# Top-k attention and SoLU MLP on one core: the verdict's product goes ahead of the last four weight products, and these are cut into two column halves

## The chip, the cores and the metric

One core of a Trainium2 chip runs the whole program, once per launch. The metric is the device time of one execution in microseconds (us); a run's time is a little longer than the span of the profile, which goes from the first to the last of the program's own instructions.

## The reference

The inputs are q, k and v of shape (8 batches, 8 heads, 576 positions, 64), two weight matrices `moe_w_in` (512 x 1024) and `moe_w_out` (1024 x 512), and a gain vector.

```python
scores = scale * np.matmul(q, k.transpose(0, 1, 3, 2))
kth = np.partition(scores, -top_k, axis=-1)[..., -top_k:-top_k + 1]   # top_k = 32
scores = np.where(scores >= kth, scores, -1000000000.0)
attn = softmax(scores);  o = np.matmul(attn, v)
x = o.transpose(0, 2, 1, 3).reshape(4608, 512)
h = x @ w_in
solu = h * softmax(h)
ln = (solu - mean(solu)) / np.sqrt(var(solu) + 1e-06) * g_ln
out = ln @ w_out                                                      # 4608 x 512
```

`softmax` and `mean` stand here for the lines that the reference writes out. All of it is in single precision.

## The kernel before

The program has two paths. The fast path computes everything with a threshold search in place of an exact selection of the 32 largest scores. It collects seven conditions that must hold for its numbers to be valid (`w_passed`, L2643, one column of the tile `ok` each). At its end `w_verdict` (L2657) adds the columns with a TensorE product (`tp_ok`, L2659), and two small VectorE instructions (L2661, L2662) make the integer `bad`. Then every engine loads `bad` into a register (`values_load`, L2710) and branches on it (`tc.If`, L2712): with zero, the general path, some thousands of instructions long, is jumped over. With these inputs it is jumped over.

The attention part works in 32 steps over batches and query tiles of 128, and the MLP in 36 tiles of 128 tokens: four per batch, and one for the 64 last positions of two batches each. The stages of a token tile are work items with these names: `mm1` (x times `w_in`, L2567), `hexp`, `solu`, `square`, `spread`, `ln`, `transpose_ln` and `copy_ln` (which give `lnT`, the normalised tile transposed, L2617 and L2623), `mm2` in two items of four products each (L2628: `lnT` chunk c times the 128 rows c of `w_out`, eight products that add up in one PSUM bank `o_ps` of 128 x 512), `store` (ScalarE copies the bank to `osb`, L2635) and `send` (SyncE issues the DMA to the output, L2639). A tile of last positions is sent with two DMAs of 64 rows, since its rows belong to two batches. The last tile of the program is of this kind.

The order of the work is not that of the loops. `work_of` lists all items with a duration, what they come after and the buffers they use; `arranged` places them on the engines by that list and a table of ranks (`PLACES`), and returns them in order of their start. The program is then written in this order, each engine's instructions in its own queue. The tile framework adds the semaphore waits: an instruction that reads a tile waits for the earlier ones that wrote it, and an engine's semaphore is counted up by the last of a run of products rather than by each. In the order that results before the change, the last items on TensorE are the two `mm2` items of the last tile and then `w_verdict`; ScalarE ends with `store`, and SyncE with the two DMAs of `send`, after which come the load of `bad`, the branch and the program's closing instructions (L2712 and L2739).

Buffers that matter here: `o_ps` has two banks (`ps_o`), `osb` has one buffer (`p1`), and `tp_ok` takes one of the two `tp` banks.

Of the kernel before, what the change touches and what calls it, by code (L numbers as in the profile page):

```python
# [699 lines left out]
def arranged(work, rank):  # L700
    ops = work.ops
    prio = {k: rank(k) for k in ops}
    number = {k: n for n, k in enumerate(ops)}
    left = {k: len(set(o["after"])) for k, o in ops.items()}
    users = {k: [] for k in ops}
    still = {}
    for k, o in ops.items():
        for a in set(o["after"]):
            users[a].append(k)
        for u in set(o["uses"]):  # L710
            still[u] = still.get(u, 0) + 1
    free = {tag: [0] * n for tag, n in work.room.items()}
    ends = {}
    ready = dict.fromkeys(ops, 0)
    idle = dict.fromkeys(ENGINES, 0)
    waiting = {e: [] for e in ENGINES}
    for k, o in ops.items():
        if left[k] == 0:
            waiting[o["engine"]].append(k)
    held = {"DVE": 0, "POOL": 0}  # L720
    mode = "f"
    start = {}
    choice = {}
    while len(start) < len(ops):
        for e in ENGINES:
            if e in choice:
                continue
            found = []
            for k in sorted(waiting[e], key=lambda k: (prio[k], number[k]))[: 10 if e == "SP" else None]:
                s = max(idle[e], ready[k])  # L730
                if ops[k]["port"]:
                    s = max(s, held["POOL" if e == "DVE" else "DVE"])
                wanted = {}
                for u in ops[k]["uses"]:
                    if u not in ends:
                        wanted.setdefault(u[0], set()).add(u)
                for tag, us in wanted.items():
                    if len(free[tag]) < len(us):
                        break
                    at = free[tag][len(us) - 1]  # L740
                    s = max(s, at + HOP[e] if at else 0)
                else:
                    found.append((s, k))
            if found:
                soon = min(found, key=lambda x: x[0])[0] + PATIENCE[e]
                choice[e] = min(
                    (prio[k] + (TURNING if e == "PE" and ops[k]["mode"] != mode else 0), number[k], s, k)
                    for s, k in found if s <= soon
                )[2:]
        s, n, e = min((choice[e][0], n, e) for n, e in enumerate(ENGINES) if e in choice)  # L750
        k = choice[e][1]
        o = ops[k]
        if e == "PE":
            s += TURN.get((mode, o["mode"]), 0)
            mode = o["mode"]
        if o["port"]:
            held[e] = s + o["ns"]
        start[k] = s
        idle[e] = s + o["ns"]
        end = s + o["late"]  # L760
        for u in set(o["uses"]):
            if u not in ends:
                free[u[0]].pop(0)
            ends[u] = max(ends.get(u, 0), end)
            still[u] -= 1
            if still[u] == 0:
                free[u[0]] = sorted(free[u[0]] + [ends[u]])
        waiting[e].remove(k)
        for j in users[k]:
            other = ops[j]["engine"]  # L770
            ready[j] = max(ready[j], idle[e] if e == other == "PE" else end + HOP[other])
            left[j] -= 1
            if left[j] == 0:
                waiting[other].append(j)
        choice = {}
    return sorted(start, key=lambda k: (start[k], number[k]))
# [1007 lines left out]
def fast_path(  # L1784
# [25 lines left out]
    nc = tc.nc  # L1810
    B, H, S, D = q.shape
    NTOK, DM = out.shape
    DFF = moe_w_in.shape[1]
    NM = 4
# [4 lines left out]
    NF = DFF // P  # L1819
# [47 lines left out]
    parts = const.tile([P, 2, NT], F32, tag="parts", name="parts")  # L1867
# [9 lines left out]
    sum_all = const.tile([P, NTT], F32, tag="sum", name="sum_all")  # L1877
# [3 lines left out]
    w_out = const.tile([P, NF, DM], F32, tag="w_out", name="w_out")  # L1881
# [17 lines left out]
    def once(d, key, make):  # L1899

        if key not in d:
            d[key] = make()
        return d[key]
# [720 lines left out]

    def mm2(d, half):
        o = once(d, "o", lambda: ps_o.tile([P, 512], F32, tag="o", name="o_ps"))
        for c in range(half * NM, (half + 1) * NM):
            nc.tensor.matmul(  # L2628
                out=o, lhsT=d["lnT"][:, c, :], rhs=w_out[:, c, :],
                start=(c == 0), stop=(c == NF - 1),  # L2630
            )

    def store(d):
        d["osb"] = p1.tile([P, DM], F32, tag="osb", name="osb")
        nc.scalar.copy(out=d["osb"], in_=d["o"])  # L2635

    def send(d):
        for rows, dst in d["stores"]:
            nc.sync.dma_start(out=dst, in_=d["osb"][rows, :])  # L2639

# [26 lines left out]
    work, order_of_tokens = work_of(B, NP, steps, NF, w_wide)  # L2669
    tokens = []  # L2670
    for b, t, _, _ in order_of_tokens:
        rows = out[b * S : b * S + SM, :].rearrange("(p t) m -> p t m", t=NM)
        d = {"sum": sum_all[:, len(tokens) : len(tokens) + 1]}
        if t < NM:
            d["x"] = lambda b=b, t=t: xs["m", b, t // 2][:, :, t % 2 * P : (t % 2 + 1) * P]
            d["stores"] = [(slice(0, P), rows[:, t, :])]
        else:
            d["x"] = lambda b=b: xs["t", b // 2]
            d["stores"] = [
                (slice(m * ST, (m + 1) * ST), out[bb * S + SM : (bb + 1) * S, :])  # L2680
                for m, bb in enumerate((b - 1, b))
            ]
        tokens.append(d)
# [5 lines left out]
        chosen_sum, kth, kth_size, ends,  # L2689
        keep, inverse, spread_r, copy_s, turn_r, copy_r, rd_out, rd_in, transpose_p, copy_p, copy_pt, transpose_last, copy_last, attn_v, attn_t,  # L2690
        copy_v, mm1, hexp, solu, square, spread, ln, transpose_ln, copy_ln, mm2, store, send, load_g, turn_g,
        copy_g, load_w, w_bits, w_corr, w_sum, w_copy, w_gain, w_again, w_exp, w_check, w_passed,
        w_verdict,
    )}
    E = mybir.EngineType
    with tc.manual_schedule(engines={E.PE, E.Activation, E.DVE, E.Pool}):
        for kind, *args in arranged(work, place_of):
            if kind in TOKEN_KINDS:
                args[0] = tokens[args[0]]
            makers[kind](*args)  # L2700


@with_exitstack
def kernel(ctx: ExitStack, tc: tile.TileContext, *args):

    nc = tc.nc
    keep = ctx.enter_context(tc.tile_pool(name="keep", bufs=1))
    bad = keep.tile([1, 1], I32, tag="bad", name="bad")
    fast_path(tc, *args, bad)
    failed = nc.values_load(bad[0:1, 0:1], min_val=0, max_val=1,  # L2710
                            skip_runtime_bounds_check_because="a comparison's result")
    with tc.If(failed > 0):  # L2712
        general_path(tc, *args)
# [30 lines left out]
```

## Time and profile before

| | |
|---|---|
| three runs | 1193.06, 1195.21 and 1195.10 us (median 1195.1) |
| the profiled execution's own time | 1193.35 us |
| its span | 1191.5 us |
| mean granted TensorE clock | 0.991 |
| TensorE products busy | 1143.5 us, 96% of the span |
| VectorE busy | 1054.0 us, 88% |
| ScalarE busy | 1014.4 us, 85% |
| GpSimd busy | 154.4 us, 13% |
| `mm2` (L2628) on TensorE | 258.2 us in 576 products of 128x512 |
| `store` (L2635) on ScalarE | 21.1 us in 36 copies, 587 ns each |

A row of the timeline or of a group gives the engine, the line of the kernel, the operation, the tile written and the tiles read, and then partitions x elements. "Busy" of an engine does not count DMA issues, register loads, branches and semaphore waits; these are shown with a q behind the engine's name (SPq). The span is 1.85 us shorter than the profiled execution's own time; that part lies outside the program's own instructions.

### The profile page before, as it was taken

How to read it: one execution, taken by the hardware profiler on the slowest of the kernel's cores; microseconds unless marked ns; L12 is line 12 of the kernel's file. 1: busy time of each engine (PE TensorE's matmuls, PEld its weight loads, DVE VectorE, ACT ScalarE, POOL GpSimd, SP SyncE). 2: the span in 40 equal slices, each digit the busy share in tenths (PEclk: the TensorE clock that was granted, in tenths of full speed). 3: DMA queues.
4: the chain of work that ended last, by engine and by line, in shares of the span. 5: the costliest groups of instructions: out<-in, count | busy, mean ns of one | idle time of the engine just before them, and what ended most of it. 6: DMA issues, size and time to landing. Idle time of an engine off the chain costs nothing.

```text
span 1191.5 us, 18863 instructions
## 1 busy us (share of the span) xinstructions
PE 1143.5 (96%) x5868; PEld 648.2 (54%) x5868; DVE 1054.0 (88%) x3113; ACT 1014.4 (85%) x2180; POOL 154.4 (13%) x169
## 2 busy tenths in 40 slices
PE   6689999999999999999999999999999999999997
PEld 3345455555555555555555655555555555555553
DVE  4999999999899999899979998899989888999821
ACT  7899798999988898999896998999877989988642
POOL 1101101102021020202031010211013001120110
PEclk9799999999999999999999999999999999999999
DMA  7323111012110122111120112111020101102521
GB/s 202 97 75 92 43 34 48 13 49 54 59 26 28 33 63 65 37 45 40 51 54 12 40 49 68 31 41 52 30 76 18 42 21 40 59 11 91 173 76 30
DMA packets 110408, 64.55 MB, mean 54 GB/s; under 512 B 89421, under 2 KB 97882, under 8 KB 110298
## 3 DMA queue, kind: packets, MB, share of 16 engines
q1 hardware_dynamic: 110298, 63.25, 18.8%
q8 instruction: 49, 0.80, 0.3%
q14 instruction: 61, 0.50, 0.1%
HBM read 53.65 MB, written 9.57 MB: 53 GB/s over the span
## 4 chain that ended last, share of the span: by engine, by line
PE 50%; DVE 27%; ACT 17%; issue 3%; POOL 2%; DMA 0%; DVEq 0%; ACTq 0%; POOLq 0%
PE o_ps L2628 14%; PE h_ps L2567 9%; PE s_ps L2216 9%; ACT sg L2291 7%; PE tp_p L2470 6%; PE om L2526 6%; DVE junkv L2234 6%; DVE w L2323 5%; DVE w L2312 5%; DVE E L2393 3%; ACT PT L2483 2%; DVE solu L2586 2%; ACT X L2227 2%; PE tp_ln L2617 2%; PE om L2535 2%
## 5 line engine op out<-in xcount | busy, mean ns | idle before, releaser
L2628 PE MATMUL o_ps<-w_out,lnT 128*128 128x512 f32 x576 | 258.2, 594 | 0.2
L2567 PE MATMUL h_ps<-w_in,xTm 128*128 128x512 f32 x512 | 229.2, 593 | 0.0
L2323 DVE MAX8 w<-w 128x8 f32<-128x288 f32 x576 | 223.3, 445 | 0.2
L2291 ACT ACTIVATE sg<-X,t 128x576 bf16<-128x576 f32 x256 | 196.4, 774 | 12.0 <-DVE t L2276 10.8
L2312 DVE SCALAR_TENSOR_TENSOR w<-X,al,sg 128x576 f32<-128x576 f32 x256 | 200.7, 813 | 0.8
L2393 DVE SCALAR_TENSOR_TENSOR E<-X,kth,E 128x576 f32<-128x576 f32 x256 | 199.1, 815 | 1.6
L2227 ACT ACTIVATE X<-s_ps 128x576 f32<-128x576 f32 x256 | 160.2, 661 | 25.0 <-PE s_ps L2216 22.5
L2234 DVE TENSOR_SCALAR_CACHE_REDUCE junkv<-X,t 128x576 bf16<-128x576 f32 x216 | 174.6, 808 | 7.6 <-ACT X L2227 1.5
L2216 PE MATMUL s_ps<-kT,qT 64*128 64x288 f32 x1024 | 169.1, 438 | 9.8 <-ACT X L2227 4.4
L2628 PEld LDWEIGHTS o_ps<-w_out,lnT 128*128 128x128 f32 x576 | 105.1, 190 | 112.4 <-issue 110.1
L2470 PE MATMUL tp_p<-ident,E 128*128 128x128 f32 x1024 | 153.1, 278 | 7.9 <-DVE E L2393 2.9
L2483 ACT COPY PT<-tp_p 128x512 f32<-128x512 f32 x256 | 147.0, 591 | 12.4 <-PE tp_p L2470 11.9
L2470 PEld LDWEIGHTS tp_p<-ident,E 128*128 128x128 f32 x1024 | 116.3, 141 | 65.4 <-issue 31.8
L2348 ACT ACTIVATE E<-X 128x1152 f32<-128x1152 f32 x128 | 149.1, 1183 | 1.4 <-PE tp_p L2470 1.2
L2567 PEld LDWEIGHTS h_ps<-w_in,xTm 128*128 128x128 f32 x512 | 93.3, 190 | 98.1 <-issue 95.7
L2526 PE MATMUL om<-PT,vm 128*64 128x320 f32 (+1 forms) x1024 | 136.1, 411 | 1.0 <-ACT osb L2635 0.9
L2186 POOL TENSOR_TENSOR zs<-zs,phalf 128x9 f32<-128x9 f32 x32 | 63.6, 1989 | 520.2 <-DVE zs L2180 520.2
L2216 PEld LDWEIGHTS s_ps<-kT,qT 64*128 64x128 f32 x1024 | 85.7, 186 | 68.3 <-issue 22.2
L2526 PEld LDWEIGHTS om<-PT,vm 128*64 128x64 f32 x1024 | 69.9, 136 | 54.6 <-issue 10.6
L2602 POOL TENSOR_SCALAR var<-var 128x1 f32<-128x1 f32 x36 | 13.0, 361 | 490.3 <-ACT e_sb L2596 490.1
L2596 ACT ACTIVATE e_sb<-solu,nmu 128x1024 f32<-128x1024 f32 x36 | 41.5, 1153 | 23.1 <-DVE nmu L2590 21.8
L2578 ACT ACTIVATE e_sb<-h_ps 128x1024 f32<-128x1024 f32 x36 | 36.7, 1020 | 20.0 <-PE h_ps L2567 19.7
(146 smaller groups left out, 1503.9 us busy)
## 6 DMA issues: line engine op xcount, KB each, us to landing
km<-in_k_dram SPq DMA_DIRECT2D x32, 256.0 KB
q_sb<-in_q_dram SPq DMA_DIRECT2D x64, 128.0 KB
vm<-in_v_dram SPq DMA_DIRECT2D x32, 256.0 KB
out_dram<-osb SPq DMA_DIRECT2D x32, 256.0 KB
scales<-rows SPq DMA_DIRECT2D x58, 128.0 KB
w_raw<-in_moe_w_in_dram SPq DMA_DIRECT2D x8, 512.0 KB
w_raw<-in_moe_w_out_dram SPq DMA_DIRECT2D x8, 512.0 KB
w_again<-in_moe_w_in_dram SPq DMA_DIRECT2D x8, 512.0 KB
```

The costliest lines, as they stand in the source:

```text
L2216: nc.tensor.matmul(out=s[:, n, 0:SH], lhsT=queries_of(i, t)[hd, :], rhs=kT[hd, k0 : k0 + SH], start=True, stop=True,)
L2227: nc.scalar.activation(out=x, in_=st[i].pop(("s", j))[:, :, 0:SH], func=AF.Copy, scale=scale,)
L2234: nc.vector.tensor_scalar(out=junk, in0=x_of(i, j), scalar1=st[i][t][:, j : j + 1], scalar2=None, op0=ALU.is_ge, op1=ALU.add, accum_out=co ...
L2291: nc.scalar.activation(out=d["sg", j], in_=x_of(i, j), func=AF.Sign, scale=-(1.0 + 2.0**-23), bias=d["t1"][:, j : j + 1], accum_out=column ...
L2312: nc.vector.scalar_tensor_tensor(out=w, in0=x_of(i, j), scalar=d["al"][:, j : j + 1], in1=d.pop(("sg", j)), op0=ALU.subtract, op1=ALU.mult,)
L2323: nc.vector.max(w8[:, j, 8 * half : 8 * half + 8], w[:, half * SH : (half + 1) * SH])
L2393: nc.vector.scalar_tensor_tensor(out=e, in0=x_of(i, j), scalar=d["kth"][:, j : j + 1], in1=e, op0=ALU.is_ge, op1=ALU.mult, accum_out=den_a ...
L2470: nc.tensor.transpose(tp[:, c, :], e[:, c * P : (c + 1) * P], ident)
L2483: nc.scalar.copy(out=dst, in_=st[i].pop(("tp", j)))
L2526: nc.tensor.matmul(out=o[h * D : (h + 1) * D, cols], lhsT=vm[:, h, c, :], rhs=pt[:, h * NM + c, :], start=(c == 0), stop=False,)
L2567: nc.tensor.matmul(out=h[:, half, :], lhsT=x[:, c, :], rhs=w_in[:, c, half * 512 : (half + 1) * 512], start=(c == 0), stop=(c == NP - 1),)
L2628: nc.tensor.matmul(out=o, lhsT=d["lnT"][:, c, :], rhs=w_out[:, c, :], start=(c == 0), stop=(c == NF - 1),)
```

## The change

Three things are changed, all at the end of the program. `w_verdict` is taken out of its place in the order and put ahead of the last `mm2` item, the one with the last four products. In that item each of the four products of 512 columns becomes two of 256: first the four of columns 0 to 255, then the four of columns 256 to 511. For that tile `store` makes two copies of 256 columns, and behind each of them in the program stand the DMAs of that column half, so there are four DMAs of 64 rows x 256 columns where there were two of 64 x 512. All other tiles have one part and keep their form.

```diff
     def mm2(d, half):
         o = once(d, "o", lambda: ps_o.tile([P, 512], F32, tag="o", name="o_ps"))
-        for c in range(half * NM, (half + 1) * NM):
-            nc.tensor.matmul(
-                out=o, lhsT=d["lnT"][:, c, :], rhs=w_out[:, c, :],
-                start=(c == 0), stop=(c == NF - 1),
-            )
+        parts = d["parts"] if half else [slice(0, DM)]
+        for m in parts:
+            for c in range(half * NM, (half + 1) * NM):
+                nc.tensor.matmul(
+                    out=o[:, m], lhsT=d["lnT"][:, c, :], rhs=w_out[:, c, m],
+                    start=(c == 0), stop=(c == NF - 1 and m == parts[-1]),
+                )
 
     def store(d):
         d["osb"] = p1.tile([P, DM], F32, tag="osb", name="osb")
-        nc.scalar.copy(out=d["osb"], in_=d["o"])
+        for m in d["parts"]:
+            nc.scalar.copy(out=d["osb"][:, m], in_=d["o"][:, m])
+            if len(d["parts"]) > 1:
+                out_of(d, m)
+
+    def out_of(d, m):
+        for rows, dst in d["stores"]:
+            nc.sync.dma_start(out=dst[:, m], in_=d["osb"][rows, m])
 
     def send(d):
-        for rows, dst in d["stores"]:
-            nc.sync.dma_start(out=dst, in_=d["osb"][rows, :])
+        if len(d["parts"]) == 1:
+            out_of(d, d["parts"][0])
...
-        d = {"sum": sum_all[:, len(tokens) : len(tokens) + 1]}
+        d = {"sum": sum_all[:, len(tokens) : len(tokens) + 1], "parts": [slice(0, DM)]}
...
-        for kind, *args in arranged(work, place_of):
+        order = [k for k in arranged(work, place_of) if k[0] != "w_verdict"]
+        last = max(n for n, k in enumerate(order) if k[0] == "mm2")
+        tokens[order[last][1]]["parts"] = [slice(0, DM // 2), slice(DM // 2, DM)]
+        order.insert(last, ("w_verdict", 0))
+        for kind, *args in order:
```

## The prediction

> **What bounds the kernel now.** TensorE is busy for 96% of the span, but the change touches only the last 10 us, so I read the end of the profile. First the chain of waits over the last 20 us:
>
> ```profile
> 1172.97 0.87 PE tp_ln L2617 x8
> 1173.85 10.32 PE o_ps L2628 x24
> 1184.16 0.03 ACTq L2635
> 1184.19 0.04 issue
> 1184.23 0.59 ACT osb L2635
> ```
>
> TensorE runs 24 products on end and only the copy of the last bank follows. But the span ends at 1191.5, 6.7 us after this copy, and none of that counts as busy. So the second view is the timeline after 1184:
>
> ```profile
> 1184.08 0.19 PE L2659 MATMUL tp_ok<-ok,ones 128*1 128x7 f32 x2
> 1184.23 0.59 ACT L2635 COPY osb<-o_ps 128x512 f32<-128x512 f32 x1 [6.33 <-PE o_ps L2628]
> 1184.31 0.15 DVE L2661 TENSOR_REDUCE n_ok<-tp_ok 1x1 f32<-1x7 f32 x1 [8.87 <-PE tp_ok L2659]
> 1184.50 0.14 DVE L2662 TENSOR_SCALAR bad<-n_ok 1x1 int32<-1x1 f32 x1
> 1184.84 1.13 SPq L2639 DMA_DIRECT2D out_dram<-osb  x2
> ```
>
> `bad` is there at 1184.64, before the copy ends. Third, the lines of the register load (L2710), the branch and its landing (L2712), and the closing (L2739):
>
> ```profile
> L2710 ACTq TENSOR_LOAD <-bad x1: 462/462/462, 1184.7 to 1184.7; - x1
> L2710 SPq TENSOR_LOAD <-bad x1: 848/848/848, 1186.0 to 1186.0; - x1
> L2712 SPq EVENT_SEMAPHORE  x8: 17/17/17, 1189.6 to 1190.2; - x8
> L2712 DVEq EVENT_SEMAPHORE  x1: 21/21/21, 1189.1 to 1189.1; - x1
> L2712 PEldq EVENT_SEMAPHORE  x1: 51/51/51, 1189.8 to 1189.8; - x1
> L2739 SPq DRAIN x3: 7/7/13, 1190.7 to 1191.1; - x3
> ```
>
> The columns after x are shortest, median and longest ns, then first and last start. All engines but SyncE load `bad` at 1184.7. SyncE is at 1186.0 only, because its two DMA issues stand ahead in its queue. It branches until 1187.0, goes on at 1189.62 (2.6 us later), steps through 16 semaphore waits until 1190.7, and the closing barrier, in which all others already stand, ends the span. So the path that sets the end is: last product, copy, SyncE's issues (1.13), load (0.85), branch and restart (2.7), closing (1.9). The verdict isn't on it: `bad` had been ready for 1.39 us when SyncE came to read it.
>
> **The change part by part.**
>
> *The verdict earlier.* Its last input, a column of `ok`, is written at 1175.4, and the item would now stand near 1182.4, so it waits for nothing, and `bad` comes some 1.7 us earlier. VectorE and GpSimd, idle by then, branch earlier; ScalarE and TensorE can't before their last copy and products; none of the four ends the span. Gain on the path: nothing. The cost is on TensorE: two tiny products between full ones. Three rows price it. `tp_ok` starts 0.52 us after the last full product (1183.56 to 1184.08), where full ones follow at 0.429: 0.09. Its second pass starts 0.03 later. And the first full product after tiny ones pays for an uncovered weight load:
>
> ```profile
> 1057.97 0.16 PE L2172 MATMUL est<-stats,qTt 128*128 128x1 bf16 x1
> 1058.00 2.39 PE L2628 MATMUL o_ps<-w_out,lnT 128*128 128x512 f32 x5
> ```
>
> Five products take 2.39 us where 4 x 0.429 + 0.592 makes 2.31: 0.08, and it starts 0.03 after the tiny one. Sum 0.23 us; bounds 0.06 (the two tiny steps alone) and 0.4 (also a bare load of 0.19). At the end, where `tp_ok` stood, nothing is saved: the copy waited for the product before it.
>
> *The halves.* Products of 128x256 follow each other at 0.215 us in the trace (`om` L2535), so eight take 1.72 us and four full ones 1.72: zero. What should bring something is that the first half's copy starts while the second half is computed. The changed program, built but not run, says no: it gives the first 256-column copy a wait on TensorE's count after the eighth product, and the second copy no wait on TensorE. The semaphore is counted up only at the last of the eight. So the first copy starts where the full one did. A shorter copy is a gain all the same:
>
> ```profile
> L2635 ACT COPY osb<-o_ps 128x512 f32<-128x512 f32 x36 | 21.1, 587 | 24.6 <-PE o_ps L2628 18.6 <-issue 6.0
> L2509 ACT COPY PT<-tp_pt 128x256 f32<-128x256 f32 x32 | 12.2, 380 | 1.9 <-PE tp_pt L2505 1.9
> ```
>
> The first DMA may be issued 587 - 380 = 0.21 us earlier. The second copy ends some 0.25 later (copies of 512 columns follow at 0.47) and hides behind SyncE's first two issues.
>
> *Four DMAs.* SyncE issued the two 64-row DMAs in 0.49 and 0.59 us with 0.055 between them, and other pairs of such stores show 0.495 to 0.540 and 0.590 to 0.596. That an issue of 64 rows doesn't shrink with its bytes shows in the loads of 64 rows x 256 B (L2044: median 0.547 of 64). Two more are 2 x (0.59 + 0.055) = 1.29, and a separate wait ahead of the third 0.05: 1.34. Behind them in SyncE's queue wait its load of `bad` and its branch, and all engines wait for these in the barrier. Bounds: 0.8 (at the shortest store issue, 0.343) to 1.4.
>
> The Trainium skill prices this otherwise: "DMA: Bandwidth & Descriptors", section "Anatomy of one DMA — SWDGE (gpsimd) path", puts the sequencer's dispatch at about 50 ns of a fixed 2 us per DMA, for another issuing path. By that two more issues are 0.1 and the whole sum would be about 0.2 us. The trace's 0.49 and 0.59 per issue on SyncE say otherwise, and I go by them.
>
> *What comes after.* SyncE's load of `bad` (0.85) could come down to the 0.46 of ScalarE, which had no DMA ahead: 0 to -0.39; I take 0, because SyncE again comes from its own issues. The restart after the branch took 2.6 us on SyncE and 3.3 to 4.4 on the others, so I leave it; the earlier branches of two engines may relieve it by some tenths, not counted.
>
> *Sum:* 0.23 - 0.21 + 1.34 = +1.4 us (bounds 0.06 - 0.21 + 0.8 - 0.39 = +0.3 and 0.4 - 0.21 + 1.4 = +1.6). The profiled execution would go from 1193.35 to 1194.7. The four known times of before (1193.06, 1193.35, 1195.10, 1195.21) spread over 2.1 us, and the profiled one is 1.75 below the median of the runs. I lay the sum on the mean of the four, 1194.2: 1195.6.
>
> **The rivals.** A measurement of this kernel can tell about 0.2%, 2.4 us, from no change.
>
> *The last store decides (slower).* SyncE's closing waits include the stores' arrival. In the trace's semaphore updates the first store is complete at 1187.39 and the second at 1189.59, 2.2 us apart, and SyncE read that semaphore at 1189.71: 0.12 us to spare. If each further store adds 2.2, the fourth arrives at 1187.45 + 6.6 = 1194.05, and with the 1.6 us of closing after it the span ends at 1195.7: +4.2, profiled 1197.5. It decides from an arrival after 1191.2, about 4.4 us after the fourth issue; from 1192.2 on the kernel is slower beyond 0.2%. For it: only stragglers made the second store late, and there will be twice as many packets. Against: the bytes are the same, and at half the spacing the fourth store arrives at 1190.8, which costs nothing.
>
> *The halves do overlap.* Then the first copy starts four products (0.86) earlier, SyncE issues the first pair during the second half, and the third issue starts at about 1185.2: the issues end at 1186.4 in place of 1186.0, +0.5 us. Against it stands the built program's wait. The Trainium skill, "PSUM — Partial Sum Buffer", section "PSUM bank collisions raise a hardware error", says that an engine's read and TensorE's write of one bank must be kept apart even at other columns, which speaks against this overlap too; no run here shows it.
>
> *The tail shrinks (faster).* If SyncE's load falls to 0.46 and the earlier branches of the others save it up to half of its 2.6 us restart, the sum is 1.4 - 0.4 - 1.3 = -0.3. Even this stays within 0.2%; to be faster by 2.4 us, 3.8 would have to vanish from a tail of 7.3.
>
> **How the numbers follow.** My forecast 0.58, of which 0.03 comes out beyond 0.2% by the scatter of the runs; the late store 0.22; overlap 0.05; the shrunken tail 0.08; anything else 0.07, split 0.05 faster and 0.02 slower. So slower 0.03 + 0.22 + 0.02 = 0.27, same 0.55 + 0.05 + 0.08 = 0.68, faster 0.05. The range goes from the lowest time of before with the lower bound of the sum (1193.06 + 0.3 = 1193.4) to the mean with the late store's whole price (1194.2 + 4.2 = 1198.4).
>
> **What would show it.** In the changed profile: the first 256-column copy starts after the eighth short product; the eight together take 1.7 us; `tp_ok` opens a gap of about 0.2 us in the row of products; SyncE shows four issues over 2.4 us, its load of `bad` starts about 3.0 us after the end of the last product in place of 1.9, and its first L2712 wait comes 2.6 us after its branch. The prediction is wrong if the first copy starts 0.9 us before the last product ends, if the issues get shorter with the rows' bytes, or if a closing wait of SyncE stands for longer than 17 ns, which is the late store.

## The result, and the profile after

The changed kernel takes 1196.59 us against 1194.38 us, medians of 19 runs each. The ratio is 1.0015, with a 95% interval of 1.0008 to 1.0022: 1.8 us slower, between 1.0 and 2.6 (the medians differ by 2.2). One run of the changed kernel, of 1662.57 us at a granted clock of 0.654, counts in its median and not in the ratio. The profiled execution of the changed kernel took 1194.25 us, its span is 1192.5 us and its granted clock 0.990. It is the quickest of the 19, 0.9 us ahead of the next. The rows below are those of this execution; what the others lost beyond it can't be seen in them.

The lines below answer to those shown of before. First the end of the chain of waits of the changed kernel (start in us, length in us, what):

```profile
1172.68 0.87 PE tp_ln L2617 x8
1173.55 6.87 PE o_ps L2630 x16
1180.42 0.12 PE tp_ok L2668 x2
1180.54 3.67 PE o_ps L2630 x16
1184.21 0.03 ACTq L2638
1184.24 0.04 issue
1184.28 0.37 ACT osb L2638
```

`tp_ok` now stands inside the row of products, and the first 256-column copy starts behind all sixteen passes of the short products, not behind eight of them. From the first of the last eight transposes to the first copy it is 1184.28 - 1172.68 = 11.60 us; before it was 1184.23 - 1172.97 = 11.26. I call the stretch from that transpose to the end of the span the tail. With the spans to the hundredth, as the traces have them, it is 1192.46 - 1172.68 = 19.78 us after and 1191.54 - 1172.97 = 18.57 before, 1.2 us more. (The expectations below say 18.5 for before, from the rounded span.)

The timeline of the same stretch, with the DMA issues, which the chain leaves out:

```profile
1178.54 1.88 PE L2630 MATMUL o_ps<-w_out,lnT 128*128 128x512 f32 x4
1180.35 0.19 PE L2668 MATMUL tp_ok<-ok,ones 128*1 128x7 f32 x2
1180.47 3.72 PE L2630 MATMUL o_ps<-w_out,lnT 128*128 128x256 f32 x16
1184.28 0.65 ACT L2638 COPY osb<-o_ps 128x256 f32<-128x256 f32 x2 [6.67 <-PE o_ps L2630]
1184.67 2.47 SPq L2644 DMA_DIRECT2D out_dram<-osb  x4
```

The last product ends at 1180.47 + 3.72 = 1184.19. SyncE's issues take 2.47 us where two took 1.13; in the trace they are 0.492, 0.588, 0.605 and 0.587 long. The two copies are over at 1184.93, ahead of the third issue.

The third view is the register load (L2723), the branch and its landing (L2725) and the closing (L2752). After the x stand shortest, median and longest ns, and then first and last start in us:

```profile
L2723 PEldq TENSOR_LOAD <-bad x1: 485/485/485, 1181.0 to 1181.0; - x1
L2723 ACTq TENSOR_LOAD <-bad x1: 462/462/462, 1184.3 to 1184.3; - x1
L2723 SPq TENSOR_LOAD <-bad x1: 739/739/739, 1187.2 to 1187.2; - x1
L2725 SPq COMPARE_BRANCH  x1: 50/50/50, 1188.0 to 1188.0; - x1
L2725 SPq EVENT_SEMAPHORE  x8: 17/17/17, 1190.5 to 1191.1; - x8
L2725 PEldq EVENT_SEMAPHORE  x1: 51/51/51, 1185.3 to 1185.3; - x1
L2752 SPq DRAIN  x3: 7/7/13, 1191.6 to 1192.0; - x3
```

SyncE comes to read `bad` at 1187.2, 3.0 us after the last product, goes on behind its branch at 1190.5, and has stepped through its waits at 1191.6, where its drains begin. All other engines have landed by 1187.5 (ScalarE the last of them), so SyncE alone ends the span. TensorE read `bad` at 1181.0, when fourteen of the sixteen passes had still to start.

### The profile page after: what moved, and what is told of

It is laid out like the page before. It is cut to its first block, busy times and chain, and to the rows that moved or that the text cites. A ratio compares the mean times of both kernels' runs of the same rounds, so it can differ in the third digit from the quotient of the medians.

```text
span 1192.5 us, 18883 instructions
## 1 busy us (share of the span) xinstructions
PE 1143.6 (96%) x5876; PEld 649.7 (54%) x5876; DVE 1054.0 (88%) x3113; ACT 1013.8 (85%) x2181; POOL 154.3 (13%) x169
## 4 chain that ended last, share of the span: by engine, by line
PE 56%; DVE 22%; ACT 16%; issue 2%; POOL 2%; DMA 0%; DVEq 0%; ACTq 0%; POOLq 0%
PE o_ps L2630 15%; PE h_ps L2567 11%; PE s_ps L2216 9%; PE tp_p L2470 7%; PE om L2526 6%; ACT sg L2291 6%; DVE junkv L2234 5%; DVE w L2312 4%; DVE w L2323 4%; DVE E L2393 3%; PE tp_ln L2617 2%; ACT PT L2483 2%; PE om L2535 2%; ACT X L2227 2%; DVE solu L2586 2%
## 5 line engine op out<-in xcount | busy, mean ns | idle before, releaser
L2630 PE MATMUL o_ps<-w_out,lnT 128*128 128x512 f32 (+1 forms) x584 | 258.5, 588 | 0.3
L2348 ACT ACTIVATE E<-X 128x1152 f32<-128x1152 f32 x128 | 149.1, 1183 | 1.4 <-PE tp_p L2470 1.2
```

Source lines behind the costliest of these rows:

```text
L2630: nc.tensor.matmul(out=o[:, m], lhsT=d["lnT"][:, c, :], rhs=w_out[:, c, m], start=(c == 0), stop=(c == NF - 1 and m == parts[-1]),)
```

## The experiments

Every kernel is the changed one with the edit shown, unless it says otherwise, and was timed in five rounds against the kernel before, in three batches on three chips, each with its own runs of before. The tail is the stretch defined above, from one profiled execution.

| kernel | ratio to before, 95% interval | tail, us |
|---|---|---|
| before | 1 | 18.6 |
| the change | 1.0015 [1.0008, 1.0022] | 19.8 |
| verdict moved, whole parts | 1.0002 [0.9993, 1.0011] | 18.9 |
| halves, verdict in its old place | 1.0008 [0.9999, 1.0017] | 20.7 |
| quarters | 1.0032 [1.0021, 1.0043] | 23.6 |
| halves, two stores of whole rows | 0.9999 [0.9990, 1.0008] | 18.8 |
| halves in two banks | 0.9998 [0.9989, 1.0007] | 18.5 |
| one store on each queue | 1.0005 [0.9996, 1.0014] | 18.7 |
| the same, verdict moved | 0.9999 [0.9990, 1.0008] | 18.3 |
| two banks, one store of each half on each queue | 1.0001 [0.9992, 1.0010] | 18.1 |
| both stores from ScalarE | 1.0001 [0.9992, 1.0010] | 18.5 |
| the same, verdict moved | 0.9992 [0.9983, 1.0001] | 18.1 |
| two banks, all four stores from ScalarE, verdict moved | 0.9988 [0.9979, 0.9997] | 17.9 |
| no branch | 0.9972 [0.9962, 0.9982] | 15.9 |

**The verdict alone.** The parts are left whole:

```diff
-        tokens[order[last][1]]["parts"] = [slice(0, DM // 2), slice(DM // 2, DM)]
```

> Only the verdict is moved ahead of the last four weight products; these keep their 512 columns, and there is one copy and two DMAs as before. The tail is measured from the start of the last eight transposes (tp_ln) to the end of the span: 18.5 us before, 19.8 after the whole change. My theory: the verdict is not on the path that sets the end, so its place brings nothing by itself. It costs TensorE 0.3 us between the products, and the earlier branches of VectorE and GpSimd give back up to 0.26 (SyncE's register load and restart were 0.11 and 0.15 shorter in the changed profile): tail 18.4 to 18.8, time within 0.5 us of before. Rival, the verdict's place alone makes the loss: tail 19.5 or more. Rival, the early verdict is a real gain that the halves throw away: tail below 18.0.

The two ends of the stretch, from the chain of waits of this kernel:

```profile
1173.42 0.87 PE tp_ln L2617 x8
1185.00 0.58 ACT osb L2638
```

From the last eight transposes to the copy it took 11.58 us, 0.32 more than before, and the tail grew by the same 0.3, to just above what was expected. The end of SyncE's row, from the groups of this kernel:

```profile
L2722 SPq TENSOR_LOAD <-bad x1: 850/850/850, 1186.8 to 1186.8; - x1
L2724 SPq COMPARE_BRANCH  x1: 50/50/50, 1187.7 to 1187.7; - x1
L2724 SPq EVENT_SEMAPHORE  x8: 17/17/17, 1190.4 to 1190.9; - x8
```

Load and restart are those of before (0.85 us, and 2.6 from the branch to the first wait behind it). That TensorE, VectorE and GpSimd read `bad` and branch 3.4 us earlier, counted from the last eight transposes, gives SyncE nothing. So this part costs only its gap in the row of products, about a quarter of the loss, which the times alone don't tell from nothing.

**The halves alone.** The verdict goes back to its place:

```diff
-        order = [k for k in arranged(work, place_of) if k[0] != "w_verdict"]
+        order = list(arranged(work, place_of))
...
-        order.insert(last, ("w_verdict", 0))
```

> Only the halves: the last four weight products in 256-column halves, two copies, four DMAs; the verdict stays behind the last product. My theory: two more DMA issues on SyncE (1.34) less the shorter first copy (0.21): tail 18.5 + 1.1 = 19.6, time +1.1 us on before. The first copy starts after the last product as in the whole change. Rival (the loss comes from the verdict's place): tail 18.5. Rival (the last store's arrival decides): one of SyncE's closing waits is longer than 17 ns, and the tail is over 20.

The tail was 20.7, a microsecond over what was expected, and one row says where it lies (timeline of this kernel):

```profile
1184.25 3.60 SPq L2644 DMA_DIRECT2D out_dram<-osb  x4
```

Three of the four issues took 0.492, 0.588 and 0.547 us, the fourth 1.774, about 1.2 too much. The other terms came out as expected. In the times (1.0008) no extra microsecond shows, but they don't exclude one, and this execution (1195.03 us) was quicker than the median of its kernel (1195.49). Whether the other runs have the long issue too is not known. The last section comes back to it.

**Quarters.** If the issues behind the last copy carry the loss, four more of them should cost about as much each:

```diff
-        tokens[order[last][1]]["parts"] = [slice(0, DM // 2), slice(DM // 2, DM)]
+        tokens[order[last][1]]["parts"] = [slice(n * P, (n + 1) * P) for n in range(4)]
```

> The whole change with four column quarters instead of two halves: 128-column products, four copies, eight DMAs of 64 rows x 128 columns. A dose for the price of a DMA issue. My theory: an issue costs SyncE 0.59 + 0.055 us whatever its bytes, so four more issues and two more separate waits add 4 x 0.645 + 0.1 = 2.7, the first copy is 0.08 shorter: tail 19.8 + 2.6 = 22.4, time about +2.6 us on the changed kernel. Rival (an issue costs by its bytes, total bytes being the same): tail 19.8. Rival (the last store's arrival decides, 2.2 us per store): tail 26 or more, with a long closing wait on SyncE.

The kernel was 3.8 us slower than before, where the halves cost 1.8. Its issues in the timeline:

```profile
1186.03 6.00 SPq L2644 DMA_DIRECT2D out_dram<-osb  x8
```

Six more issues than before take 6.00 - 1.13 = 4.87 us. One of them lasted 1.50; without its extra 0.9 that is 0.66 for each. The tail is 1.2 over what was expected: the long issue is 0.9 of that, and a restart of 2.73 us most of the rest. Rows of 512 bytes cost SyncE what rows of 2 KB do. The price is that of these stores of 64 rows: the stores of whole tiles, 128 rows and twice the bytes, were issued in 0.34 to 0.37 us in 27 of 32 cases in the kernel before, the others in 0.45 to 0.60. The same run speaks on the stores' arrival: by the trace's semaphore updates the eight stores are complete between 1187.95 and 1193.34, 2.3 us before SyncE lands behind its branch at 1195.66. More stores don't arrive later than SyncE gets there, because SyncE itself is later.

**Halves without the extra stores.** Both copies are kept, and two DMAs of whole rows follow the second:

```diff
         for m in d["parts"]:
             nc.scalar.copy(out=d["osb"][:, m], in_=d["o"][:, m])
-            if len(d["parts"]) > 1:
-                out_of(d, m)
...
-        if len(d["parts"]) == 1:
-            out_of(d, d["parts"][0])
+        out_of(d, slice(0, DM))
```

> The whole change, but behind the two half copies stand two DMAs of the full width, as before the change, in place of four. My theory: this takes back the 1.34 of two issues, and the first issue comes 0.27 later, after both copies: tail (start of the last eight transposes to the end of the span; 18.5 before, 19.8 after, 18.9 with the verdict alone moved) 18.9 to 19.0, time within 1 us of before. SyncE's register load should be 0.85 again if it goes by the stores behind which it stands (two of 2 KB rows), 0.74 if it goes by something else in the change. Rival (the split copies or products are what costs): tail 19.5 or more.

With verdict and halves in place and only the two added DMAs gone, the loss is gone within the interval: 0.9999, and a tail 0.3 over that of before, as with the verdict alone. The timeline row and the load of this kernel:

```profile
1186.36 1.13 SPq L2642 DMA_DIRECT2D out_dram<-osb  x2
```

```profile
L2720 SPq TENSOR_LOAD <-bad x1: 840/840/840, 1187.5 to 1187.5; - x1
```

The load is at 0.84 again. It was 0.84 to 0.85 in the three kernels whose last stores have rows of 2 KB (before and the verdict alone are the others), and 0.73 to 0.74 in the four with narrower rows on SyncE, whether the verdict stood early or late: the 0.11 us that the change wins here come with its stores ahead of the load. These are narrower and there are more of them, and no run separates the two.

**A bank for each half.** Now the first copy really may start early, since the second half adds up in another PSUM tile. All eight products of the last tile are cut into halves here, not the last four alone:

```diff
-        o = once(d, "o", lambda: ps_o.tile([P, 512], F32, tag="o", name="o_ps"))
-        parts = d["parts"] if half else [slice(0, DM)]
-        for m in parts:
+        once(d, "o", lambda: ps_o.tile([P, 512], F32, tag="o", name="o_ps"))
+        if len(d["parts"]) > 1:
+            once(d, "o2", lambda: ps_big.tile([P, 2, 512], F32, tag="big", name="o2_ps"))
+        for n, m in enumerate(d["parts"]):
+            o = d["o2"][:, 0, :] if n else d["o"]
...
-                    start=(c == 0), stop=(c == NF - 1 and m == parts[-1]),
+                    start=(c == 0), stop=(c == NF - 1),
...
-            nc.scalar.copy(out=d["osb"][:, m], in_=d["o"][:, m])
+            o = d["o2"][:, 0, :] if m.start else d["o"]
+            nc.scalar.copy(out=d["osb"][:, m], in_=o[:, m])
```

> The whole change, but all eight products of the last tile are made in column halves, and the second half adds up in a PSUM bank of its own, so that the first copy waits for the products of its own half alone. It should start 1.7 us before the last product ends (eight passes of 0.215 us). My theory: SyncE then issues the first two DMAs under the second half, and behind the second copy stand two issues as before the change: the 1.34 is gone, but nothing is won, because the number of issues after the last copy is that of before: 18.5 + 0.34 (verdict between the products) - 0.21 (shorter last copy) - 0.26 (relief as in the changed profile) = 18.4, between 18.2 and 18.7. Rival (the wait of the first copy is not what made the change lose): tail 19.5 or more. Rival (overlap is worth what it hides, 1.7 us): tail below 17.5.

The timeline of this kernel, copies and issues:

```profile
1182.91 0.37 ACT L2641 COPY osb<-o_ps 128x256 f32<-128x256 f32 x1 [4.96 <-PE o_ps L2632]
1183.31 2.92 SPq L2647 DMA_DIRECT2D out_dram<-osb  x4
1184.59 0.37 ACT L2641 COPY osb<-o_ps 128x256 f32<-128x256 f32 x1 [1.31 <-PE o_ps L2632]
```

The first copy starts 1.7 us before the second, and two issues are done by 1184.5. Yet the second pair can't be issued before the second copy, and it is two issues of 64 rows again: 0.47 and 0.72 us. What stands behind the last product is what stood there before, so the kernel is as fast as before (0.9998). The overlap repays the added issues and no more.

**One of the two stores on ScalarE's queue.** The verdict in its old place and whole parts, as before the change, but the second store is issued by the engine that made the copy:

```diff
         for rows, dst in d["stores"]:
-            nc.sync.dma_start(out=dst[:, m], in_=d["osb"][rows, m])
+            eng = nc.scalar if d.get("last") and rows.start else nc.sync
+            eng.dma_start(out=dst[:, m], in_=d["osb"][rows, m])
...
-        order = [k for k in arranged(work, place_of) if k[0] != "w_verdict"]
+        order = list(arranged(work, place_of))
...
-        tokens[order[last][1]]["parts"] = [slice(0, DM // 2), slice(DM // 2, DM)]
-        order.insert(last, ("w_verdict", 0))
+        tokens[order[last][1]]["last"] = True
```

> The kernel before with one thing changed: of the last tile's two DMAs SyncE issues the first and ScalarE the second, behind its copy. The issue is taken off SyncE's queue, the opposite of what the change does. My theory: SyncE's queue before its register load is what the end waits for, so the tail is 0.59 + 0.055 = 0.64 shorter: 17.9, time -0.6 us. Rival (something behind SyncE's issues sets the end, such as the last store's arrival or ScalarE's own branch): tail 18.3 or more.

This missed: 18.7 where 17.9 was expected. The issue is saved (SyncE has one, of 0.49 us), and what it saved is given back behind it, in the load and the restart:

```profile
L2723 SPq TENSOR_LOAD <-bad x1: 1097/1097/1097, 1186.1 to 1186.1; - x1
```

```profile
L2725 SPq COMPARE_BRANCH  x1: 50/50/50, 1187.3 to 1187.3; - x1
L2725 SPq EVENT_SEMAPHORE  x8: 17/17/17, 1190.4 to 1191.0; - x8
```

The load takes 1.10 us where 0.85 was, and from the branch to the first wait it is 3.1 us where 2.6 was. In this kernel the five engines branch within 1.5 us (1186.0 to 1187.4). I therefore suspected that engines that restart together hold each other up.

**The same with the verdict moved**, so that three engines have branched long before:

```diff
-            nc.sync.dma_start(out=dst[:, m], in_=d["osb"][rows, m])
+            eng = nc.scalar if d.get("last") and rows.start else nc.sync
+            eng.dma_start(out=dst[:, m], in_=d["osb"][rows, m])
...
-        tokens[order[last][1]]["parts"] = [slice(0, DM // 2), slice(DM // 2, DM)]
+        tokens[order[last][1]]["last"] = True
```

> one_store_each with the verdict ahead of the last four weight products. In one_store_each SyncE saved an issue but its register load took 1.10 (0.85 before) and its restart after the branch 3.1 (2.6 before), while all five engines branched within 1.5 us. My theory: loads and restarts of engines that branch together slow each other; with the verdict early VectorE, GpSimd and TensorE are through before SyncE and ScalarE branch, so SyncE's restart is 2.5 to 2.7 and the tail (start of the last eight transposes to the end of the span; 18.5 before, 18.7 in one_store_each) 18.2 to 18.5 in spite of 0.34 more on TensorE. Rival (ScalarE's own issue and branch beside SyncE's are what slow it): restart 3.0 or more, tail 18.9 to 19.1.

```profile
L2724 SPq TENSOR_LOAD <-bad x1: 1066/1066/1066, 1187.4 to 1187.4; - x1
```

```profile
L2726 SPq COMPARE_BRANCH  x1: 50/50/50, 1188.6 to 1188.6; - x1
L2726 SPq EVENT_SEMAPHORE  x8: 17/17/17, 1191.1 to 1191.6; - x8
```

These groups show 2.45 us for the restart again, with TensorE, VectorE and GpSimd through by 1187.4. That is what the theory of the crowding asked for, on one execution of each kernel; the last section has rows of ScalarE that don't fit it. The load stays at 1.07, so it is not the crowd of branches that slows it. In both kernels ScalarE issues a store at the same moment and loads `bad` within 0.08 us of SyncE. Which of the two slows the load stays open.

**Two banks, and one store of each half on each queue**, with the verdict in its old place: the edit of "a bank for each half" and

```diff
-            nc.sync.dma_start(out=dst[:, m], in_=d["osb"][rows, m])
+            eng = nc.scalar if d.get("last") and rows.start else nc.sync
+            eng.dma_start(out=dst[:, m], in_=d["osb"][rows, m])
...
-        order.insert(last, ("w_verdict", 0))
+        tokens[order[last][1]]["last"] = True
```

with the order as arranged.

> A version meant to beat both: column halves with a PSUM bank for each, so that the first half is copied and stored under the second; SyncE and ScalarE issue one DMA of each half; the verdict stays behind the last product. Behind the last copy stands one issue per engine. My theory: against before, the last copy is 0.21 shorter and one issue (0.64) is gone from SyncE's queue; no product stands between the weight products: tail 18.5 - 0.85 = 17.7, time -0.8 us. Against it, ScalarE's first issue (0.5) stands before its second copy only if that copy could start earlier, which it can't: the products of the second half last 1.7 us. Rival (the arrival of the stores sets the end once SyncE is earlier): tail 18.0 to 18.5.

A single issue of 0.49 us is left behind the last copy on SyncE. The load took 0.92 and the restart 2.97, with all five engines branching between 1185.5 and 1186.4; the tail is 18.1 against the 17.7 expected, and the times show nothing (1.0001). The same miss as with one store on each queue, from the same two terms.

**Both last stores on ScalarE's queue**, verdict in its old place:

```diff
-            nc.sync.dma_start(out=dst[:, m], in_=d["osb"][rows, m])
+            (nc.scalar if d.get("last") else nc.sync).dma_start(out=dst[:, m], in_=d["osb"][rows, m])
...
-        order = [k for k in arranged(work, place_of) if k[0] != "w_verdict"]
+        order = list(arranged(work, place_of))
...
-        tokens[order[last][1]]["parts"] = [slice(0, DM // 2), slice(DM // 2, DM)]
-        order.insert(last, ("w_verdict", 0))
+        tokens[order[last][1]]["last"] = True
```

> The kernel before, but both DMAs of the last tile are issued by ScalarE behind its copy, none by SyncE. SyncE loads the verdict as soon as it is there (1184.7 in the time of before), branches by 1185.3 and restarts by 1188.6 at the latest. My theory: then SyncE no longer leads; ScalarE's restart (copy end, two issues 1.13, load 0.5 to 0.85, branch and 2.6: about 1189.4) and the stores' arrival (1189 to 1189.6) do, and SyncE's 16 closing waits (about 1.1) and the barrier (0.8) come behind the arrival: end at 1190.8 to 1191.3, tail 17.9 to 18.4. Rival (SyncE's closing waits run while the stores are under way): tail 17.3 or less. Rival (it doesn't matter which engine issues): tail 18.5.

SyncE, with no issue ahead, loads `bad` in 0.47 us together with the others, and is at its closing waits at 1188.2 (groups of this kernel):

```profile
L2722 SPq TENSOR_LOAD <-bad x1: 472/472/472, 1184.0 to 1184.0; - x1
L2722 ACTq TENSOR_LOAD <-bad x1: 762/762/762, 1185.4 to 1185.4; - x1
```

```profile
L2724 SPq COMPARE_BRANCH  x1: 50/50/50, 1184.5 to 1184.5; - x1
L2724 SPq EVENT_SEMAPHORE  x8: 17/17/17, 1188.2 to 1189.4; - x8
```

The eight waits now spread over 1.2 us, not 0.6. Between them lies a gap of 0.8, until the second store is complete at 1188.97, 4.2 us after its issue; from there the closing takes 1.85. Here a store's arrival does set the end. The tail of 18.5 is that of before, just above what was expected.

**The same with the verdict moved:**

```diff
-            nc.sync.dma_start(out=dst[:, m], in_=d["osb"][rows, m])
+            (nc.scalar if d.get("last") else nc.sync).dma_start(out=dst[:, m], in_=d["osb"][rows, m])
...
-        tokens[order[last][1]]["parts"] = [slice(0, DM // 2), slice(DM // 2, DM)]
+        tokens[order[last][1]]["last"] = True
```

> act_stores with the verdict ahead of the last four weight products: ScalarE issues both DMAs of the last tile, SyncE none, and SyncE, VectorE, GpSimd and TensorE branch and restart under the last products. In act_stores SyncE stood in a closing wait until the second store arrived (1188.97), 4.2 us after its issue, and 1.85 us of closing followed. My theory: with no other restart under way the stores arrive 2.0 to 2.6 us after their issue, and ScalarE's restart takes 2.5; ScalarE's arrival in the barrier is then last: tail 17.6 to 18.1 (18.5 before), time -0.4 to -0.9 us. Rival (the arrival stays at 4 us): tail 18.8. Here the verdict's early place would be worth something for the first time.

The tail was 18.1, the upper end of what was expected, though the stores did not arrive as expected: they were issued at 1185.04 and 1185.64 and complete at 1188.83 and 1189.13, again 3.5 to 3.8 us later and not 2.0 to 2.6, and ScalarE landed behind its branch at 1189.81, so both were late together. The ratio, 0.9992, doesn't exclude 1.

**Two banks on top of that**, with the verdict moved and all four stores on ScalarE's queue: the edit of "a bank for each half" and

```diff
-            nc.sync.dma_start(out=dst[:, m], in_=d["osb"][rows, m])
+            (nc.scalar if d.get("last") else nc.sync).dma_start(out=dst[:, m], in_=d["osb"][rows, m])
...
+        tokens[order[last][1]]["last"] = True
```

> act_stores_verdict_early with column halves in two PSUM banks: ScalarE issues the first half's two DMAs under the second half's products and the second half's two behind its second copy. Against act_stores_verdict_early the last copy is 0.21 shorter and its bytes are half. My theory: tail 0.2 below that kernel's, 17.4 to 17.9 (18.5 before), time -0.6 to -1.1 us: the version that could beat both. Rival (four DMAs on one queue cost again): ScalarE's second copy comes late by the first two issues, if these (1.13) do not fit between the first copy's end and the last product's (1.4): then tail 18.0 or more.

This one is faster than before by a little: 1192.63 us in the median against 1194.40, ratio 0.9988 [0.9979, 0.9997], an interval that ends just short of 1 and is the best of twelve tried with the branch. Its tail is 0.7 shorter. ScalarE's row in its timeline:

```profile
1183.06 0.37 ACT L2641 COPY osb<-o_ps 128x256 f32<-128x256 f32 x1 [4.96 <-PE o_ps L2632]
1183.46 1.60 ACTq L2647 DMA_DIRECT2D out_dram<-osb  x2
1185.10 0.37 ACT L2641 COPY osb<-o_ps 128x256 f32<-128x256 f32 x1 [1.67 <-PE o_ps L2632]
1185.51 1.22 ACTq L2647 DMA_DIRECT2D out_dram<-osb  x2
```

Its landing and SyncE's, from the groups of this kernel:

```profile
L2729 SPq EVENT_SEMAPHORE  x8: 17/17/17, 1185.8 to 1189.5; - x8
L2729 ACTq EVENT_SEMAPHORE  x1: 17/17/17, 1190.1 to 1190.1; - x1
```

SyncE has done its load, branch and landing by 1185.8 and only waits for the stores, the last of them complete at 1189.25; the waits that it still has to step through then last until 1190.1. ScalarE is later by some 0.1 us, at 1190.14, but from there to the end of the span it is 0.9 us, where it is 1.9 from SyncE's landing when SyncE is the last: ScalarE has one wait to step through, SyncE sixteen. One issue of the first pair took 1.00 us and held the second copy back: it starts at 1185.10, 0.40 after the last product's end, where the change has 0.08. Without that issue there may be a little more in it.

**No branch.** Last, what the end of this program costs whatever stands ahead of it. From the kernel before, with the verdict in its old place and whole parts, the general path with its register load and branch is left out; the verdict is computed and not used:

```diff
-    failed = nc.values_load(bad[0:1, 0:1], min_val=0, max_val=1,
-                            skip_runtime_bounds_check_because="a comparison's result")
-    with tc.If(failed > 0):
-        general_path(tc, *args)
```

> The kernel before without its general path, the register load and the branch: the verdict is computed and not used. It prices the end of the program. My theory: SyncE goes from its two issues straight to the closing waits, where it stands until the stores arrive, 2.0 to 2.6 us after the second issue without restarts beside them, and 1.85 of closing follow: the end comes 0.55 (second issue's start after the first) + 2.0 to 2.6 + 1.85 = 4.4 to 5.0 after SyncE's first issue, where it was 6.7: tail 18.5 - 2 = 16.3 to 16.9, time -1.7 to -2.3 us. Rival (the restart hides under the stores' arrival): tail 18.0 or more.

It gains 3.3 us, more than the 1.7 to 2.3 expected, and now SyncE's issues are followed by nothing but the stores' arrival (timeline, and waits of SyncE after 1183, with the us in total, the count and the longest):

```profile
1184.49 1.13 SPq L2644 DMA_DIRECT2D out_dram<-osb  x2
```

```profile
SPq L2746 <- DMA out_dram<-osb: 1.7, 1, 1.7
```

The stores are complete 2.3 and 2.4 us after their issues began, at 1186.76 and 1187.40, and 1.1 us of closing follow, where 1.85 was expected. Without the branch the kernel would end on its stores; with it, load, restart and eight more waits take longer than they do. So the end of the program costs more than any order of the last items gave back.

## Why the prediction was right, point by point

The sum was +1.4 us. The runs give +1.8 [1.0, 2.6], the two profiled tails +1.2, and the time of 1196.59 lies in the range, 1.0 over the 1195.6 that was forecast. Term by term, from the two profiles:

| term | predicted | measured |
|---|---|---|
| last transposes to first copy | +0.23 | 11.26 to 11.60: +0.34 |
| first copy's start to first issue | -0.21 | 0.61 to 0.39: -0.22 |
| issues | +1.34 | 1.13 to 2.47: +1.34 |
| SyncE's load of `bad` | 0 | 0.85 to 0.74: -0.11 |
| branch to first wait | 0 | 2.62 to 2.47: -0.15 |
| closing | 0 | 1.93 to 1.93: 0 |
| sum | +1.4 | +1.2 |

**The issues** are the loss. The kernel with two whole stores shows it by taking them away, and quarters by adding four. That they came out to the hundredth as priced in this execution is luck, since executions of other kernels here show issues of 1.0 to 1.8 us. The other terms, +0.11 on the gap and -0.26 on load and restart, partly cancel, which is luck too. The Trainium skill's 50 ns in "DMA: Bandwidth & Descriptors", section "Anatomy of one DMA — SWDGE (gpsimd) path", is stated for another issuing path and is not the price of an issue on SyncE's queue: here each of the four held it for 0.49 to 0.61 us.

**The gap on TensorE** was mis-sized, inside its bounds: 0.34 for 0.23. The gap ahead of `tp_ok` was the 0.09 predicted (the last full pass starts 0.52 ahead, where passes follow at 0.43), its second pass came 0.03 later as said, but the first short pass then starts 0.10 after it, not 0.03, and costs 0.10 more than those that follow, not 0.08. The row that I borrowed had one tiny product of another kind ahead of it.

**The short products** are where the working was wrong without harm. Each single precision product is two passes in the profile: the 576 rows of the table of before are 36 tiles of eight products. So eight short products take some 3.45 us (3.72 with the first one's delay and the end of the last, in the row above), not 1.7, and the four full ones that they replace as much. Both sides of that term were halved alike, and it stayed zero by luck. But `bad` came 3.4 us earlier (8.23 us after the last eight transposes began, where it was 11.67), not 1.7, and in the rival of the overlap the first copy would be about 1.7 us earlier, not 0.86, as the kernel with two banks shows.

**Who branches early.** I wrote that TensorE can't branch before its last products. It did: it read `bad` at 1181.0 and came to the branch at 1181.5, 2.7 us before its last product ended, and ScalarE read it during its last copies. In these rows the load and the branch ran ahead of products and copies that stood before them in the program. That cost the sum nothing, since SyncE was last in any case.

**Load and restart** gave 0.26 us together, where I had taken nothing. The load goes with the stores ahead of it, as told above. The restart of SyncE, when it is the last to branch, measured 2.45 to 2.73 in the kernel before and in six others here, with the verdict early or late. The 0.15 are inside that scatter, and I put them down to nothing. That it costs microseconds at all fits the Trainium skill, "Runtime: NRT & Kernel Launch", section "Instruction fetch mechanics": a taken branch to a target outside the prefetched window stalls for a fetch of it. Here the jump passes over the whole general path. The DMA views show ten packets on the instruction queues from 1184 to the end in the kernel before, and none from 1176 on in the kernel without the branch; that SyncE's restart is the wait for them is not shown.

**The rivals.** The late store did not come. By the semaphore updates of the changed kernel the four stores are complete at 1188.79, 1188.95, 1189.17 and 1189.43, 0.16 to 0.26 apart and not 2.2, and SyncE read the last of them 1.36 us after. With both stores on ScalarE's queue it did decide, once SyncE was no longer late itself, so the mechanism exists; for this order its chance of 0.22 looks too high, since each added issue makes SyncE some 0.65 later, more than the stores' spacing. My sign for it was wrong too: SyncE's wait on one semaphore is a row of 17 ns however long it waited, and the waiting stands as a gap ahead of the row. A row that waits on two semaphores can be long, as the one of 1.7 us in the kernel without the branch. The overlap didn't happen, as the built program's wait had said; and had it happened, the kernel with two banks says that it would have ended level. Of the shrunken tail only the 0.26 us above came.

## What to carry to other kernels

Look for the engine that ends the span, and count every instruction in its queue behind the last result: at 0.5 to 0.6 us each, splitting a store to start it earlier loses unless the added issues lie beside work that is still running. A split in columns gives no overlap while both parts add up in one tile with one wait; with a tile of its own for each part the added issues were hidden, but a gain came only when all of them also left the queue of SyncE, which has sixteen closing waits, for that of ScalarE, which has one, with the verdict early. Before a term is borrowed from a row of the trace, check how many rows one instruction of the program makes.

## What was not expected of the hardware

- One DMA issue among many took 1.0 to 1.8 us instead of 0.5 to 0.7: the fourth of the halves alone (1.77), the fifth of the quarters (1.50), and the second on ScalarE's queue with two banks (1.00). All three began while a 16 KB packet of an instruction queue (q8 in the traces) was under way, and ended 0.3 to 0.4 us after it. Of the issues behind the first 20 us of all fourteen traces, 93 of the 99 longer than 0.9 us overlap such a packet, and 345 of the 6625 others do. That the fetch is what holds them up is likely by this, but no run shows it.
- SyncE lands later when it branches together with others. Its restart took 2.97 to 3.61 us in the three kernels where three or more other engines branch within 1.3 us of it (one store on each queue, two banks with one each, both stores from ScalarE), against 2.45 to 2.73 where at most one does. In two more kernels it can't be read, because SyncE's first wait behind the branch is there for a store. ScalarE doesn't follow: its restart took 2.67 in the halves alone, with three others within 0.1 us, and 3.01 with two banks, with none within 1.3.
- The same register load took 0.47 us on SyncE with no DMA issue ahead, 0.73 to 0.74 behind four or eight narrow stores of its own, 0.84 to 0.85 behind two wide ones, and 0.92 to 1.10 where ScalarE issued stores and loaded beside it.
